# Network 1's last two blocks take seven block products for eight, and attention goes four heads by 512 tokens

## The chip, the cores and the metric

One core of a Trainium2 chip runs the whole program. The metric is the device time of one execution in microseconds (us); the median of three runs stands for a kernel. PE is TensorE, DVE VectorE, ACT ScalarE, POOL GpSimd, and SP the engine whose queue issues all transfers here.

## What is computed

```python
scores = scale * np.matmul(q_c, k_c.transpose(0, 1, 2, 4, 3))   # chunks of 64 tokens, 8 x 8 heads, head size 64
attn = softmax(scores)                                        # row maximum taken off, 1e-9 in the sum
x = np.matmul(attn, v_c)                                      # 4608 tokens x 512 after the transpose of heads
h = x @ w_in; r = np.maximum(h, 0.0); x = (r * r) @ w_out     # network 1, 512 -> 2048 -> 512
h = x @ w_in2                                                 # network 2, same sizes
g = (a0 + a1*h + a2*h**2 + a3*h**3) / (1 + |b0|*|h| + |b1|*h**2 + 1e-6)
out = g @ w_out2
```

## The kernel before

**Numbers and products.** All data is float32. Every operand of a large product is held as two parts, `hi` (rounded to fp32r) and `lo` (what is left), and `mm3` (L372 to L376) issues three matmuls of 128x512 for one product of parts: lo by hi, hi by lo, hi by hi. Making the two parts of a tensor costs a copy (`copy`, L198 on ACT, L200 elsewhere) and a subtraction (`split_lo`, L203).

**Steps.** The 4608 tokens are 9 blocks of 512 (`NBLK`), the 2048 columns of the middle are 16 tiles of 128 (`NF`). One step s is one block and one such tile. In the loop of network 1 a step is `mm_h` (four chunks of 128 of the 512 inputs by three matmuls, 12 in all, into a PSUM bank `h`), `act1` (relu and square on ACT, then `gh`, a copy, and `gl`, a subtraction, both on DVE as a rule), and two and a half steps later `mm_out1` (12 matmuls into the four banks `ACC`). The tile `r` between the square and the subtraction has one buffer, so that the next step's relu waits for this step's `gl`. There are two `h` banks. After 16 steps `evac1` copies the four banks out and `store1` writes them to DRAM.

**Attention** is laid between the steps in units of 256 tokens by 8 heads: transposes of q and k on DVE, 64 small matmuls for the scores (`mm_s`), the softmax on DVE and ACT, eight block transposes on DVE (`s_tr`), and 64 small matmuls for the result at the next unit (`mm_pv2`), whose output is split straight into the tile X of its block. Two units make a block, in the order of the blocks, one in about 8 steps.

**An order written by hand.** Each piece of work is put down by `at(t, fn, ...)` with a time t in steps (`MOVED` shifts some); `issue` sorts by t and each engine takes its own work in that order, so the order on an engine is fixed and a wait at its head holds all that is behind it. In the stretch from step 22 on, the weights of network 2 are split on POOL and stored (`w2_split`, `w2_sum`, `w2_sum_split`, `w2_store`), one pair of tiles in 12 steps.

**The held steps.** The products h of the last 20 steps of network 1 (`BACK`) are made ahead, two steps in the time of one, and their r kept in SBUF (`keep`); their `mm_out1` comes later.

**Pairs.** The first product of network 2 is taken for two blocks at a time. A unit of a pair covers two blocks by two tiles; the 512 inputs are cut in halves too, so it is a product of 2x2 blocks, made by seven block products (`mm_p`, 6 matmuls each) on sums of x and of w (`x2q`, `w2q` in DRAM) in place of eight. `UNIT_SEQ = "1o562o37o4o"` gives a unit's order on PE; each `o` is one outstanding `mm_out` of 12 matmuls. `q_fork` copies the bank of product 1 to a second bank, `q_s5` copies that of 5 to SBUF, `q_v` and `q_22` add (L926, L930). Four tiles come out of a unit and each goes through eleven operations (`tile_jobs`: abs, lin, id, q, wh, wa, ln, exp, wr, u, g). Blocks 0 to 7 of network 2 are four pairs; block 8 goes in the plain way at the end, then 20 outstanding `o`. In this part a planner (`plan`) sets the order: it gives each job a cost (`COST`), a due time and the jobs it needs, and takes the job with the earliest due time among those ready on an engine. The weights for each `o` lie in a ring of six pages, filled by `o_load` (L275) with both parts, after the `mm_out` six `o` earlier.

## Time and profile before

| | |
|---|---|
| runs | 1602.35 us median of 3 (1601.53 to 1603.12) |
| the profiled execution | 1602.25 us; its span 1600.4 us |
| PE busy | 1587.4 us of the span |
| DVE, ACT, POOL busy | 1075.1, 921.6, 772.7 us |
| granted clock of PE | full in all 40 slices of the span |

The span runs from the first to the last instruction. A matmul's recorded duration overlaps the next one's; how often one starts says more of the rate. A row of a group of instructions gives line, engine, operation, the tile written and those read, the count, the busy time, the mean of one, and the idle time of the engine ahead of it with what ended it.

### The profile page before, as it was taken

The numbers are of one execution on the slowest core, as the hardware profiler recorded it, in microseconds if no ns is written. First come the engines' busy times: TensorE is split into PE (matmuls) and PEld (weight loads), VectorE is DVE, ScalarE is ACT, GpSimd is POOL, SyncE is SP. The second block draws the span as 40 slices with busy tenths as digits, with TensorE's granted clock in tenths as the row PEclk, the third lists the DMA queues.
The fourth block names the chain that finished last, engine by engine and source line by source line (L and its number), as shares of the span: only waits on it lengthen the run. The fifth ranks groups of instructions, "written<-read, shape, count | busy, mean of one in ns | idle before, by whom it ended". The sixth has DMA issues, their size and how long they took to land.

```text
span 1600.4 us, 25717 instructions
## 1 busy us (share of the span) xinstructions
PE 1587.4 (99%) x9165; PEld 1313.8 (82%) x9165; DVE 1075.1 (67%) x1688; ACT 921.6 (58%) x1462; POOL 772.7 (48%) x737
## 2 busy tenths in 40 slices
PE   8999999999999999999999999999999999999998
PEld 7878888888888888888888888888888888888887
DVE  6886666765666666653067887787777777777640
ACT  5863343333333333334578887887888878777641
POOL 3640212123121312224368876877687856555554
PEclk9999999999999999999999999999999999999999
DMA  9854574354535445444988999989999996666544
GB/s 251 229 146 135 179 209 119 100 141 103 155 89 140 118 125 134 134 126 133 315 308 272 291 296 328 336 279 329 338 291 279 330 344 226 204 205 211 178 162 141
DMA packets 359567, 337.28 MB, mean 211 GB/s; under 512 B 195472, under 2 KB 269456, under 8 KB 358416
## 3 DMA queue, kind: packets, MB, share of 16 engines
q1 hardware_dynamic: 359440, 335.64, 67.9%
q8 instruction: 73, 1.20, 0.3%
q14 instruction: 54, 0.44, 0.1%
HBM read 253.76 MB, written 81.79 MB: 210 GB/s over the span
## 4 chain that ended last, share of the span: by engine, by line
PE 94%; DVE 3%; SPq 1%; ACT 1%; DMA 0%; issue 0%; POOL 0%; DVEq 0%; POOLq 0%; ACTq 0%
PE acc L374 16%; PE acc L376 16%; PE acc L375 16%; PE h L374 15%; PE h L376 15%; PE h L375 15%; PE h L592 1%; PE a L571 1%; DVE w L967 1%; SPq L662 1%; DVE spare L974 0%; DMA qn<-in_q_dram 0%; DVE w L954 0%; DVE w L950 0%; DVE h L971 0%
## 5 line engine op out<-in xcount | busy, mean ns | idle before, releaser
L374 PE MATMUL h<-x,w 128*128 128x512 f32 (+1 forms) x824 | 320.0, 388 | 0.6 <-ACT r L491 0.5
L375 PE MATMUL h<-x,w 128*128 128x512 f32 (+1 forms) x824 | 319.0, 387 | 0.3 <-DVE x L203 0.3
L376 PE MATMUL h<-x,w 128*128 128x512 f32 (+1 forms) x824 | 318.9, 387 | 0.0
L946 POOL TENSOR_TENSOR t<-t,r 128x512 f32<-128x512 f32 x144 | 188.3, 1308 | 135.1 <-ACT t L938 129.9
L374 PE MATMUL acc<-gh,w 128*128 128x512 f32 x576 | 226.2, 393 | 0.0
L376 PE MATMUL acc<-gh,w 128*128 128x512 f32 x576 | 224.3, 389 | 0.0
L375 PE MATMUL acc<-gl,w 128*128 128x512 f32 x576 | 224.2, 389 | 0.0
L374 PE MATMUL acc<-w,gl 128*128 128x512 f32 x575 | 223.7, 389 | 0.0
L375 PE MATMUL acc<-w,gh 128*128 128x512 f32 x575 | 223.7, 389 | 0.0
L376 PE MATMUL acc<-w,gh 128*128 128x512 f32 x575 | 223.7, 389 | 0.0
L203 POOL TENSOR_TENSOR gl<-spare,gh 128x512 fp32r<-128x512 f32 x146 | 191.3, 1316 | 54.3 <-ACT gh L198 48.2
L491 ACT ACTIVATE r<-h 128x512 f32<-128x512 f32 x124 | 73.8, 595 | 246.2 <-PE h L376 153.1
L200 POOL CAST st<-wc 128x512 fp32r<-128x512 f32 x32 | 21.2, 663 | 376.7 <-DVE wc L245 376.7
L374 PEld LDWEIGHTS h<-x,w 128*128 128x128 f32 x824 | 154.7, 188 | 32.7 <-ACT r L491 0.9
L375 PEld LDWEIGHTS h<-x,w 128*128 128x128 f32 x824 | 154.7, 188 | 31.9 <-DVE x L203 0.5
L376 PEld LDWEIGHTS h<-x,w 128*128 128x128 f32 x824 | 154.7, 188 | 31.6
L200 DVE CAST gh<-r 128x512 fp32r<-128x512 f32 x117 | 57.2, 489 | 149.8 <-ACT r L492 149.2
L950 DVE TENSOR_TENSOR w<-w,h 128x512 f32<-128x512 f32 x144 | 98.4, 683 | 67.1 <-ACT w L942 64.3
L374 PEld LDWEIGHTS acc<-gh,w 128*128 128x128 f32 x576 | 108.1, 188 | 23.3 <-POOL w L203 0.4
L376 PEld LDWEIGHTS acc<-gh,w 128*128 128x128 f32 x576 | 108.1, 188 | 22.7
L376 PEld LDWEIGHTS acc<-w,gh 128*128 128x128 f32 x575 | 107.9, 188 | 22.5
L374 PEld LDWEIGHTS acc<-w,gl 128*128 128x128 f32 x575 | 107.9, 188 | 22.4
(145 smaller groups left out, 3061.5 us busy)
## 6 DMA issues: line engine op xcount, KB each, us to landing
w<-w2o SPq DMA_DIRECT2D x144, 512.0 KB, 4.9
w<-w2q SPq DMA_DIRECT2D x256, 256.0 KB, 5.0
x2q<-xroom SPq DMA_DIRECT2D x24, 896.0 KB, 6.4
st<-in_moe_w_in_dram SPq DMA_DIRECT2D x32, 512.0 KB, 4.5
st<-in_moe_w_out_dram SPq DMA_DIRECT2D x32, 512.0 KB, 4.6
w2q<-st SPq DMA_DIRECT2D x32, 512.0 KB, 2.8
w<-x2q SPq DMA_DIRECT2D x30, 512.0 KB, 9.2
x<-x2q SPq DMA_DIRECT2D x26, 512.0 KB, 7.7
```

Source lines behind the costliest of these rows:

```text
L200: eng.tensor_copy(out=o, in_=x)
L203: eng.tensor_tensor(out=o, in0=x, in1=hi.bitcast(F32), op=ALU.subtract)
L374: nc.tensor.matmul(out=o, lhsT=al, rhs=bh, start=first and i == 0, stop=False, **kw)
L375: nc.tensor.matmul(out=o, lhsT=ah, rhs=bl, start=False, stop=False, **kw)
L376: nc.tensor.matmul(out=o, lhsT=ah, rhs=bh, start=False, stop=last and i == len(pairs) - 1, **kw)
L491: nc.scalar.activation(out=r, in_=ps, func=ACTF.Relu)
L571: nc.tensor.matmul(out=o[half(c), h, p], lhsT=q_[half(h), p, half(c)], rhs=k_[half(h), p, half(c)], start=True, stop=True)
L592: nc.tensor.matmul(out=o[c][half(h), i, p], lhsT=v_[half(c), 2 * p + h], rhs=a_[h][half(c), p] if t < 2 * TPB else a_[h][half(c), :, p], s ...
L662: nc.sync.dma_start(out=x[:, t], in_={"q": q, "k": k_in, "v": v}[nm][0, 4 * k:4 * k + 4, t0:t0 + 128, :].rearrange("h r d -> r h d"))
L946: nc.gpsimd.tensor_tensor(out=t, in0=t, in1=T["r", b, f], op=ALU.mult)
L950: nc.vector.tensor_tensor(out=w, in0=w, in1=T["H", b, f], op=ALU.mult)
L967: nc.vector.scalar_tensor_tensor(out=w, in0=w, scalar=co[:, 0:1], in1=T["r", b, f], op0=ALU.add, op1=ALU.mult)
```

## The change

Blocks 7 and 8 of network 1 (`NP1 = 1` pair) leave the loop of steps and become a fifth pair (`KP = 5`), the first of the planned part; their tiles get relu and square (`q_relu`, `q_sq`) instead of the eleven operations. The loop has 7 blocks, 112 steps (`NS1`), and its last 20 are the held ones. For this, network 1's first weights are needed as seven sums (`w1q`): POOL adds hi and lo together again, forms the sums and splits them, in eight portions. The input of the pair is needed unsplit in DRAM: `x1_raw` copies it out of the banks, `x1_store` writes it. The second weights of network 1 are kept as one sum (`w1r`) in place of two parts, so a ring page for a step below 144 is loaded at half the size and split again by `op_hi` (ACT) and `op_lo` (DVE). In the loop from step 30 the copy `gh` is on ACT, and the subtraction `gl` of odd steps on POOL, except where it is needed early. Attention units after the first become 512 tokens by 4 heads, 12 of them from step 29.55 to 92.55, with blocks 7 and 8 (units 28 to 34) ahead of some of the others. The last two portions of network 2's weights go into the planned part. The scratch tiles `e` share buffers with `q`, `ee` and others.

```diff
+NP1 = 1
+W2_EARLY = 6
+ATTN = [(29.55, 12), (34.55, 14), (40.55, 28), (45.55, 16), (50.55, 32), (56.55, 18), (61.55, 20), (66.55, 22), (72.55, 30),
+        (77.55, 34), (82.55, 24), (87.55, 26)]
+T_W1Q = [24 + 12 * i + x for i in range(4) for x in (4.1, 9.25)]
+T_W1R = [19.8, 21.0, 22.2, 76.1, 77.3, 78.5, 81.2, 84.0]
+GC_A = range(30, 92)
+GL_G = range(31, 92, 2)
...
+    NB1 = NBLK - 2 * NP1
+    NS1 = NB1 * NF
+    KP = NP1 + NBLK // 2
...
+    def w1q_sum(u):
+        raw = []
+        for i in range(2):
+            need("w", (0, 2 * u + i, 0), 4)
+            hi, lo = w_slot(2 * u + i, 0)
+            raw.append(tl("wc", [128, DM], I32, "wc").bitcast(F32))
+            nc.gpsimd.tensor_tensor(out=raw[i], in0=hi.bitcast(F32), in1=lo.bitcast(F32), op=ALU.add)
+        T["raw", u] = raw
...
+    def w1q_split(u, i):
+        if i:
+            st = T["sums1", u] = tl("attn", [128, DM, 2], I32, "ee")
+        x = s_view(T["sums1", u])
+        y = T.pop(("raw", u))[0].rearrange("p (k s j) -> p s k j", k=2, s=2) if i else x[:, 1].bitcast(F32)
+        copy(nc.gpsimd, x[:, 0], y)
+        split_lo(nc.gpsimd, x[:, 1], y, x[:, 0])
...
+        if NS1 - BACK + j < NS:
+            nc.sync.dma_start(out=o_page(j).bitcast(F32)[:, 1], in_=w1r[f // 2][:, f % 2])
+        else:
+            nc.sync.dma_start(out=o_page(j).bitcast(F32), in_=w2o[f // 2][:, f % 2])
+
+    def op_hi(j, eng):
+        stage("page_o", j, 0)
+        need("ring_o", j, 1)
+        copy(eng, o_page(j)[:, 0], o_page(j)[:, 1].bitcast(F32))
+
+    def op_lo(j, eng):
+        stage("page_o", j, 1)
+        o = o_page(j)
+        split_lo(eng, o[:, 1], o[:, 1].bitcast(F32), o[:, 0])
...
-        copy(on(f"gc{s}", "V"), g[0], r)
-        split_lo(on(f"gl{s}", "V"), g[1], r, g[0])
+        copy(on(f"gc{s}", "A" if s in GC_A else "V"), g[0], r)
+        split_lo(on(f"gl{s}", "G" if s in GL_G and s not in early else "V"), g[1], r, g[0])
...
+    def q_relu(b, f):
+        r = T["r", b, f] = keep("r", b * NF + f - NS1 + BACK)
+        nc.scalar.activation(out=r, in_=T.pop(("H", b, f)), func=ACTF.Relu)
+
+    def q_sq(b, f):
+        r = T.pop(("r", b, f))
+        nc.scalar.activation(out=r, in_=r, func=ACTF.Square)
...
-    for m in range(NBLK // 2):
+    for m in range(KP):
...
+        if b < NBLK:
+            e = job("A", COST["relu"], ready_, due - 20, q_relu, b, f)
+            made[b, f] = job("A", COST["sq"], [(e, 0)], due - 10, q_sq, b, f)
+            return [(e, E_LAT)]
...
+            page = [(made["ring", n], D_LAT)] if ("ring", n) in made else []
+            if N_PRE <= n and s < NS:
+                e = job("A", COST["hi"], page, due - 16, op_hi, n, nc.scalar)
+                page = [(job("V", COST["add"], [(e, E_LAT)], due - 8, op_lo, n, nc.vector), E_LAT)]
+            made[x] = job("PE", size["o"], deps + page, 0, mm_o, n)
```

**POOL in the loop of steps.** Before, the four sums of a portion of network 2's weights (L311) and the splits of the two sums, with nothing but weights around them (L200 is a copy, L203 a subtraction):

```order
L311 TENSOR_TENSOR st<-wc 128x256
L311 TENSOR_TENSOR st<-st,wc 128x256
L311 TENSOR_TENSOR st<-wc 128x256
L311 TENSOR_TENSOR st<-wc,st 128x256
L200 CAST st<-st 128x2x256
L203 TENSOR_TENSOR st<-st 128x2x256
L200 CAST st<-st 128x2x256
L203 TENSOR_TENSOR st<-st 128x2x256
```

The same place now (L386 the sums, L217 copies, L220 subtractions), with a step's `gl` inside and a portion of network 1's weights behind (L302 adds the parts, L312 forms the sums in the buffer `ee`):

```order
L386 TENSOR_TENSOR st<-wc 128x256
L386 TENSOR_TENSOR st<-st,wc 128x256
L386 TENSOR_TENSOR st<-wc 128x256
L386 TENSOR_TENSOR st<-wc,st 128x256
L217 CAST st<-st 128x2x256
L220 TENSOR_TENSOR st<-st 128x2x256
L220 TENSOR_TENSOR gl<-r,gh 128x512
L217 CAST st<-st 128x2x256
L220 TENSOR_TENSOR st<-st 128x2x256
L302 TENSOR_TENSOR wc<-w_12_88 128x512
L302 TENSOR_TENSOR wc<-w_13_89 128x512
L312 TENSOR_TENSOR ee<-wc 128x256
```

A step's `gl` now stands behind the weights' sums and their first split.

**ACT in network 1's pair.** Around the start of the pair's fifth unit (`h<-h` is `q_fork`, `s<-h` is `q_s5`, L1064 and L1068 are relu and square, `w_0<-w_0` and `w_4<-w_4` are `op_hi`, `gh<-spare` is the copy for an `o`):

```order
L1064 ACTIVATE spare_7057<-h 128x512
L1068 ACTIVATE spare_7057<-spare_7057 128x512
L215 ACTIVATE w_4_6874<-w_4_6874 128x512
L215 ACTIVATE gh<-spare_7133 128x512
L215 ACTIVATE w_0_7131<-w_0_7131 128x512
L215 ACTIVATE h<-h 128x512
L215 ACTIVATE w_0_7131<-w_0_7131 128x512
L215 ACTIVATE s_7910<-h 128x512
```

An `op_hi`, which waits for a page, now stands ahead of `q_fork`, and one ahead of `q_s5`.

**DVE in the first pair of network 2.** Before, around `q_v` and `q_22` of its third unit (L926, L930; the others are the tiles' operations):

```order
L974 SCALAR_TENSOR_TENSOR spare_8010<-h,w 128x512
L926 TENSOR_TENSOR h<-h,s_8747 128x512
L950 TENSOR_TENSOR w<-w,h 128x512
L954 SCALAR_TENSOR_TENSOR w<-w,co,h 128x512
L930 TENSOR_TENSOR h<-h,s_8747 128x512
L967 SCALAR_TENSOR_TENSOR w<-w,co,h 128x512
```

The same two sums in that pair's fourth unit now (L1056 and L1060; L220 is `op_lo`):

```order
L1112 SCALAR_TENSOR_TENSOR spare_6878<-h,w 128x512
L1056 TENSOR_TENSOR h<-h,s_9149 128x512
L220 TENSOR_TENSOR w_2_7153<-w_2_7153 128x512 x2
L220 TENSOR_TENSOR w_4_6874<-w_4_6874 128x512
L1088 TENSOR_TENSOR w<-w,h 128x512
L1060 TENSOR_TENSOR h<-h,s_9149 128x512
L1092 SCALAR_TENSOR_TENSOR w<-w,co,h 128x512
```

Three subtractions for pages stand between the two sums.

## Rows read from the trace of the kernel before

**Rows 1.** The page: busy time, share of the span and instructions of each engine.

```profile
PE 1587.4 (99%) x9165; PEld 1313.8 (82%) x9165; DVE 1075.1 (67%) x1688; ACT 921.6 (58%) x1462; POOL 772.7 (48%) x737
```

**Rows 2.** The page: the chain of work that ended last, share by engine.

```profile
PE 94%; DVE 3%; SPq 1%; ACT 1%; DMA 0%; issue 0%; POOL 0%; DVEq 0%; POOLq 0%; ACTq 0%
```

**Rows 3.** Busy time by stretch: start:end, length, engines, clock, DMA share, GB/s.

```profile
0.00:40.00 40.00, 33.53 (x448) 29.28 (x449) 27.69 (x46) 23.22 (x40) 15.02 (x19) 1.00 0.99 251
320.00:640.00 320.00, 320.00 (x2240) 265.08 (x2239) 210.58 (x374) 108.81 (x182) 74.95 (x77) 1.00 0.47 126
1520.00:1600.40 80.40, 76.27 (x340) 63.09 (x338) 19.81 (x30) 25.08 (x39) 40.39 (x38) 1.00 0.45 151
```

**Rows 4.** Who waited for whom, PE: us in total, times, longest.

```profile
PE h L374 <- DVE h L926: 1.0, 2, 0.8
PE h L374 <- ACT r L491: 0.5, 1, 0.5
```

**Rows 5.** Timeline of PE in the loop: start us, us, instruction.

```profile
332.18 0.39 PE L374 MATMUL h<-x,w 128*128 128x512 f32 x1
...
334.90 0.39 PE L374 MATMUL acc<-gh,w 128*128 128x512 f32 x1
...
337.71 1.16 PE L592 MATMUL h<-at,v 64*64 64x64 f32 x64
338.70 1.11 PE L571 MATMUL a<-k,q 64*64 64x64 f32 x64
339.74 0.50 PE L374 MATMUL acc<-gh,w 128*128 128x512 f32 x1
```

**Rows 6.** Groups of instructions by form, DVE and ACT, 320 to 640 us.

```profile
L203 DVE TENSOR_TENSOR gl<-r,gh 128x512 fp32r<-128x512 f32 x56 | 47.1, 841 | 1.9
L200 DVE CAST gh<-r 128x512 fp32r<-128x512 f32 x56 | 27.2, 485 | 71.0 <-ACT r L492 70.9
L245 DVE SCALAR_TENSOR_TENSOR wc<-wc,st 128x512 int32<-128x512 int32 x18 | 14.3, 795 | 1.1 <-ACT st L239 0.7 <-POOL st L203 0.2
L643 DVE TENSOR_TENSOR e<-e,z 128x512 f32<-128x512 f32 x14 | 12.9, 923 | 0.2
L491 ACT ACTIVATE r<-h 128x512 f32<-128x512 f32 x56 | 33.3, 595 | 124.5 <-PE h L376 73.2 <-DVE gl L203 42.1 <-issue 5.1
```

**Rows 7.** Timeline of POOL at one portion of network 2's weights.

```profile
392.82 0.84 POOL L311 TENSOR_TENSOR st<-wc 128x256 f32<-128x256 f32 x1 [11.05 <-DMA w2q<-st]
...
397.33 0.61 POOL L200 CAST st<-st 128x512 fp32r<-128x512 f32 x1
398.02 1.28 POOL L203 TENSOR_TENSOR st<-st 128x512 fp32r<-128x512 f32 x1
```

**Rows 8.** Timeline of PE just after it: the first matmul of a step's output.

```profile
404.69 0.39 PE L374 MATMUL acc<-gh,w 128*128 128x512 f32 x1
```

**Rows 9.** Busy time by stretch, first pair: one unit, four units, one unit.

```profile
797.00:817.40 20.40, 20.40 (x92) 16.89 (x91) 6.12 (x9) 12.22 (x20) 8.74 (x9) 1.00 0.95 368
817.40:899.00 81.60, 81.60 (x362) 67.57 (x361) 65.92 (x90) 66.79 (x103) 67.00 (x65) 1.00 0.86 271
919.40:939.80 20.40, 20.40 (x91) 16.89 (x91) 18.97 (x24) 15.71 (x25) 15.65 (x15) 1.00 0.91 287
```

**Rows 10.** Groups by form, DVE and ACT, 880 to 960 us.

```profile
L974 DVE SCALAR_TENSOR_TENSOR spare<-h,w 128x512 f32<-128x512 f32 x10 | 6.9, 692 | 0.3
L974 DVE SCALAR_TENSOR_TENSOR spare<-r,w 128x512 f32<-128x512 f32 x4 | 6.7, 1668 | 0.1
L971 DVE SCALAR_TENSOR_TENSOR r<-t,r 128x512 f32<-128x512 f32 x4 | 5.6, 1392 | 0.4
L198 ACT ACTIVATE gh<-spare 128x512 fp32r<-128x512 f32 x7 | 4.4, 625 | 0.0
```

**Rows 11.** The page loads (L275), 790 to 1300 us: issue to landing.

```profile
DMA to landing us min/median/max: 3.6/6.1/11.6
```

More of the change, by code (lines that the diff above doesn't have):

```diff
@@ new lines, in w1_store, with w1q_copy @@
+    def w1_store(i):
+        nc.sync.dma_start(out=w1r[i], in_=T.pop(("w1r", i)))
+    def w1q_copy(u):
+        for i in range(2):
+            need("w", (0, 2 * u + i, 0), 4)
+            for s in range(i == 0 or 2):
+                nc.sync.dma_start(
+                    out=wq[0][u][:, 2 * i + s].rearrange("p (t k j) -> p (t k) j", t=2, k=2),
+                    in_=W[0, 2 * u + i].bitcast(F32).rearrange("p t (k s j) -> p s (t k) j", k=2, s=2)[:, s])
+            stage("wq", (0, u, i), 0)
@@ L415, in w_out @@
         need("ring_o", j, 1)
+        if s < NS:
+            need("page_o", j, 2)
         stage("out_j", j, 0)
@@ L436, in mm_out2 @@
             for j in PARTS:
-                T["rest", j.start] = bank(role(NF // 2 * (NBLK // 2) - 1, "be"[j.start > 0]))
+                T["rest", j.start] = bank(role(NF // 2 * KP - 1, "be"[j.start > 0]))
                 mm3(T["rest", j.start][:, j], [(gi, [z[:, j] for z in w])], True, True)
@@ L482, in act1 @@
         ps = T.pop(("h", s))
-        r = r_p.tile([128, NB], F32, name="r", tag="r") if s < NS - BACK else keep("r", s - NS + BACK)
-        if s >= NS - BACK:
+        r = r_p.tile([128, NB], F32, name="r", tag="r") if s < NS1 - BACK else keep("r", s - NS1 + BACK)
+        if s >= NS1 - BACK:
             nc.scalar.activation(out=r, in_=ps, func=ACTF.Relu)
@@ L518, in load_tok, with load_v @@
         T[nm, t] = x
+    def load_v(t):
+        b, i = divmod(t, TPB)
+        h0 = 4 * (i // 2)
+        x = tl("attn", [128, 2, 4, D], F32, "v", f"v{t % 2}")
+        for c in range(2):
+            for off, n, bb, ss in runs(b * NB + 256 * (i % 2) + 128 * c, 128):
+                nc.sync.dma_start(out=x[off:off + n, c], in_=v[bb, h0:h0 + 4, ss:ss + n, :].rearrange("h p d -> p h d"))
+        T["v", t] = x.rearrange("p c h d -> p (c h) d")
     def load_qk(u, src, nm, hp):
@@ L614, in x2_lo, with x1_raw, x1_store @@
                     stage("x", t, i)
+    def x1_raw(c, *ts):
+        stage("xc", (ts[-1], c), 0)
+        if c == 0:
+            T["xraw"] = tl("attn", [128, 2, 512], F32, "xraw", "ee" if ts[0] == 34 else "vx")
+        x = T["xraw"].rearrange("d p (n c i) -> d c p n i", c=2, i=64)
+        copy((nc.scalar, nc.vector)[c], x[:, c], T["x2", ts[-1]][c])
+    def x1_store(*ts):
+        b, i = divmod(ts[0], TPB)
+        for c in range(2):
+            need("xc", (ts[-1], c), 1)
+        stage("x1", (b, i // 2), 0)
+        nc.sync.dma_start(out=x_rows(b)[:, i:i + 2], in_=T["xraw"])
     def s_max(t):
@@ L619, in s_max, with e_half @@
         nc.vector.tensor_reduce(out=m, in_=T["s", t], axis=AX.X, op=ALU.max)
+    def e_half(i):
+        if "ee" not in T:
+            T["ee"] = tl("attn", [128, 2, 512], F32, "ee")
+        return T["ee"][:, i]
     def s_sub(t):
@@ L1101, in attn_moe_moe_kernel @@
             break
+        before = t, t + 1
         at(t0, a_ps, t)
@@ L1130, in t_h @@
     def t_h(s):
-        return s if s < NS - BACK + 2 else NS - BACK + 2 + (s - NS + BACK - 2) * 0.5
-    for s in range(NS):
+        return s if s < NS1 - BACK + 2 else NS1 - BACK + 2 + (s - NS1 + BACK - 2) * 0.5
+    for s in range(NS1):
         if s < 2:
@@ L1146, in attn_moe_moe_kernel @@
     for i in range(NF // 2):
-        at(19.8 + 1.6 * i, w1_save, i)
+        at(T_W1R[i], w1_raw, i)
+        at(T_W1R[i] + 0.75, w1_store, i)
     for u in range(NF // 2):
+        at(20.4 + 1.6 * u, w1q_copy, u)
+        t = T_W1Q[u]
+        at(t, w1q_sum, u)
+        at(t + 0.6, w1q_sum2, u)
+        at(t + 1.2, w1q_split, u, 0)
+        at(t + 1.8, w1q_store, u, 0)
+        at(t + 2.4, w1q_split, u, 1)
+        at(t + 2.8, w1q_store, u, 1)
+    for u in range(W2_EARLY):
         t = 24.0 + 12.0 * u
@@ L1285, in x_jobs @@
+    if NP1:
+        for u in range(W2_EARLY, NF // 2):
+            w2_jobs(u, 340 * (u - W2_EARLY))
     def x_jobs(i, deps):
         m = i // 7
-        if m < NBLK // 2 and ("xq", 8 * m + 7) not in made:
+        if m < KP and ("xq", 8 * m + 7) not in made:
             later.setdefault(m, []).append((i, deps))
             return
-        deps = deps + ([(made["xq", 8 * m + 7], D_LAT)] if m < NBLK // 2 else [(made["st", NBLK - 1, k], D_LAT) for k in range(KC)])
-        due = nominal["p", m, 0, ORDER[i % 7]] if m < NBLK // 2 else nominal["s", 0]
+        deps = deps + ([(made["xq", 8 * m + 7], D_LAT)] if m < KP else [(made["st", NBLK - 1, k], D_LAT) for k in range(KC)])
+        due = nominal["p", m, 0, ORDER[i % 7]] if m < KP else nominal["s", 0]
@@ L1442, in attn_moe_moe_kernel @@
             issue(T_P2)
-        for nm, bufs in TB.items():
-            pool(ctx, "t" + nm, bufs)
         pool(ctx, "s5", 1)
@@ L1451, in attn_moe_moe_kernel @@
         T["more"] = tl("sx", [128, MORE, NB], F32, "more")
+        with ExitStack() as p2:
+            pool(p2, "w", 3)
+            pool(p2, "wc", 3)
+            issue(min(t for t, _, fn, _ in events if fn is q_abs))
+        for nm, bufs in TB.items():
+            pool(ctx, "t" + nm, bufs)
         issue(3 * NS)
```

271 lines of the change are left out of this document (180 added, 91 removed).

## The prediction

> **What bounds the kernel now.** I read the page first. PE is busy 1587.4 of 1600.4 us [rows 1], and the chain that ended last runs 94% on PE [rows 2], so the kernel is as long as PE's list of work plus its gaps. Where the 13.0 us of gaps lie is read from the busy time by stretch [rows 3]: 6.5 us in the first 40 and 4.1 in the last 80.4, none in the 320 us in the middle of network 1's loop. That leaves 2.4 us in between; the waits of PE name 1.0 of it as the sum `q_v` on DVE and 0.5 as a relu on ACT [rows 4]. So a matmul taken out of the middle is worth its full time, and any wait that is put there is paid in full. The price of a matmul is not its recorded 0.39 us: in the timeline [rows 5] twelve start between 332.18 and 334.90, 2.72 us, or 0.2267 each. The same rows give attention on PE: both products of a unit take 337.71 to 339.74, 2.03 us.
>
> The sum is made against the profiled execution, 1602.25 us, which is 0.10 below the median of the runs, 1602.35.
>
> **What goes away: 10.9 us.** Blocks 7 and 8 have 32 tiles of 12 matmuls, 384. As a pair they are 8 units of 7 products of 6, 336. The built order shows it: PE has 8015 instructions before and 7967 after, 48 fewer, and the small matmuls and transposes of attention are as many as before. 48 x 0.2267 = 10.9 us, all of it on the path, and no bank or page is added on PE's side. The attention units move earlier, and so do their 2.03 us, but they don't change.
>
> **What is added in the loop (steps 30 to 92): 0.8 us, bounds 0 to 8.** Twelve units now stand in 63 steps of 5.44 us (two times 2.72), with 24 us of attention about 367 us, where the old order gave a unit some 8 steps. DVE: of 210.6 us in 320 [rows 3] I take off the `gl`, `gh` and weight joins of rows 6 and divide by seven units: (210.6 - 47.1 - 27.2 - 14.3) / 7 = 17.4 us a unit. After: 12 x 17.4 = 209, 39 `gl` at 0.84 make 33, some 21 joins at 0.80 make 17; 259 of 367, 70% where 66% hid entirely. `gh` moves to ACT, 62 copies at 0.63 [rows 10], which brings ACT from 34% to under a half. POOL has the most to take: 23% of the time now [rows 3], which is 86 of 367 us; eight portions of `w1q` at 9.7 us (by the rows of POOL: two additions and two subtractions of 1.28, four half-size sums of 0.84, two copies of 0.61 [rows 7]), 23 `gl` at 1.28 and ten additions for `w1r` add 78, 29 and 13. That is 206, 56%. None is full; what matters is what a `gl` on POOL stands behind. At one portion of weights POOL waited 11.05 us for a store, and the first split ended at 399.3 [rows 7]. A `gl` of the third step of that portion, standing there as the order now has it, would end at 400.6, and PE took up that step's output at 404.69 [rows 8]: 4.1 us to spare. The single buffer `r` is held as long, and ACT already waited 42.1 us for it in 56 steps without PE noticing [rows 6]. On SP the loads of q and k fall from 640 to 448, and 40 transfers for `w1q` come in, 1451 instructions in all before and 1452 after; a unit's loads have about five steps, 27 us, instead of eight. I take 0.8 us, nearer to nothing, because the row has 4.1 us left; the upper bound is a POOL 5.5 us later than that at each of six portions, (5.5 - 4.1) x 6 = 8.4.
>
> **What is added in network 1's pair: 0.5 us, bounds 0 to 14.** ACT has a relu and a square where network 2 has five operations, so it has room, and DVE too. New is that `op_hi`, which waits for a page, stands in ACT's queue ahead of `q_fork`. Its load is issued after the `mm_out` six earlier, 24 matmuls or 5.4 us before product 1 ends; product 6, which needs the copy, comes 18 matmuls or 4.1 us after that. `op_hi` and `q_fork` take 0.6 us each, so PE idles only if a page lands later than 5.4 + 4.1 - 1.2 - 0.3 for the issue = 8.0 us after it is asked for. The median is 6.1, the longest 11.6 [rows 11]. Four units have this order: at worst 4 x 3.6 = 14 us. I take 0.5, as the median lies well inside.
>
> **What is added in the first pair of network 2: 1.7 us, bounds 0 to 26.** Here the last 20 outputs of network 1 meet the eleven operations on each tile, and each has an `op_hi` and an `op_lo` that the old kernel did not need. In the old first pair four units took 65.9 us of DVE and 66.8 of ACT in 81.6 [rows 9], 16.5 and 16.7 a unit of 20.4 us, and the unit before them 6.1 and 12.2. Four `op_hi` at 0.63 bring ACT to 19.2. `op_lo` subtracts two tiles of SBUF. Its nearest rows are DVE operations that read their main operands from SBUF or PSUM [rows 10]: 0.69 with one in PSUM, 1.39 and 1.67 with both in SBUF beside a busy POOL; a softmax multiplication with its main operands in SBUF took 0.92 in the loop [rows 6]. I take 1.0, so DVE needs 16.5 + 4.0 = 20.5 of 20.4: just full. A full unit was no stall at 18.97 of 20.4 [rows 9], the first of the five has 14 us free, and the pages at its start are split in the pair before. I take 1.7 us. The bounds: nothing, and five units at 18.97 + 4 x 1.67 - 20.4 = 5.25 us each, 26 us.
>
> The Trainium skill, "GPSIMD Engine Reference", section 8 (Key points), says that GpSimd shares its SBUF interfaces with VectorE and contends with DVE instructions that have two SBUF inputs. The 1.67 beside 0.69 in one stretch [rows 10] agrees with it. By that rule alone each `op_lo` costs the longer time, and the sum comes out at the first rival below.
>
> The rest is the same instructions in the same order on PE: the start, three later pairs, the last block and the end. 1602.25 - 10.9 + 0.8 + 0.5 + 1.7 = 1594.35 us, and 1594.4 for the median.
>
> **The rivals.** *DVE becomes the bound in network 2's first pair (slower).* If `op_lo` always costs 1.67, a unit needs 16.5 + 6.7 = 23.2, 2.8 over; five units lose 14 us: 1602.35 - 10.9 + 14 + 1.3 = 1606.8. It decides from 10.9 / 5 = 2.2 us a unit, an `op_lo` of 1.53 us. For it: both rows above 1.3, and the three `op_lo` between `q_v` and `q_22`, where the old PE waits already lay. Against: the unit of 18.97 contained these long operations and cost nothing, and the first unit is light.
>
> *POOL is late in the loop (no change).* With six portions each 1.4 us too late (8.4) and the other two terms (2.2), 1602.35 - 10.9 + 8.4 + 2.2 = 1602.1. For it: POOL more than doubles its work and a wait at its head holds `gl`. Against: the 4.1 us of the row, and that the steps ahead of a unit keep `gl` on DVE.
>
> *Pages land late (slower).* Four units at the longest landing: 1602.35 - 10.9 + 14 + 2.5 = 1608.0. It needs every one of them near the longest, so it is the least likely.
>
> *All of it is hidden.* No new wait, and the 0.5 us behind the relu goes because the step it hit is laid otherwise: 1602.35 - 10.9 - 0.5 = 1591.0. That is the low end of the forecast's own case, not a case of its own. That fewer matmuls are not issued is excluded by the order.
>
> **How the numbers follow.** A measurement of this kernel can tell 0.2%, 3.2 us, from no change; so faster is below 1599.1, slower above 1605.6. Forecast, new waits of up to 7 us: 0.72, all of it faster. DVE as the bound: 0.11, of which 0.03 faster, 0.02 within, 0.06 slower. POOL late: 0.11, of which 0.02 faster, 0.08 within, 0.01 slower. Pages late: 0.06, of which half within and half slower. That makes 0.77 faster, 0.13 within and 0.10 slower. The range goes from 1590.8, with every wait hidden, to 1601.5, which takes in the forecast's case and the milder part of the rivals; what is left above it is most of the 0.10 and about half of the 0.13.
>
> **What would show it.** Right: PE busy down by about 11 us in the page, the busy stretches of PE still full in the loop, PE's waits in the middle below 6 us in sum, and those there are behind DVE in network 2's first pair. Wrong in the loop: waits of PE for `gl` on POOL or for a relu on ACT behind it. Wrong in the pair of network 1: waits for `q_fork` with ACT waiting for a page. Wrong in the next pair: DVE over 95% busy in its first five units and PE waiting for `q_v` or `q_22`. If PE's busy time fell by much less than 10.9, the price of a matmul would be wrong.

## The result and the profile after

The changed kernel took 1611.9 us (median of four runs, 1609.0 to 1612.3), the kernel before 1601.95 on the same chip: ratio 1.0057, 95% interval 1.004 to 1.0075. It is slower by about 10 us, where 1594.4 was forecast and the range ended at 1601.5. The profiled execution of 1612.33 us has a span of 1610.6. In the rows, SPq stands for SP's queue of transfers, `ev`, `vx` and `xraw` for tiles that a copy out of PSUM fills.

The page of the changed kernel, busy time and the chain that ended last, which answer to [rows 1, 2]:

```profile
PE 1584.2 (98%) x9117; PEld 1305.9 (81%) x9117; DVE 1058.3 (66%) x1603; ACT 1009.0 (63%) x1612; POOL 998.8 (62%) x944
...
PE 75%; SPq 6%; POOL 5%; DMA 5%; DVE 4%; issue 3%; ACT 2%; POOLq 0%; DVEq 0%; ACTq 0%
```

The 48 matmuls are gone (9165 to 9117), but PE now idles 26.4 us instead of 13.0, and the chain leaves PE for a quarter of its length: for SP's queue, POOL, DMA and DVE. No engine but PE is over two thirds busy. So this is not a new bound, it is a set of waits. PE's busy time fell by 3.2 us only, not by 10.9; why is said with the reasons below.

Busy time by stretch after the change (columns as in [rows 3]):

```profile
160.00:320.00 160.00, 154.07 (x1137) 127.07 (x1136) 107.02 (x189) 60.88 (x103) 78.70 (x78) 0.98 0.68 184
320.00:640.00 320.00, 317.65 (x2401) 262.07 (x2400) 185.81 (x335) 156.03 (x256) 175.15 (x175) 1.00 0.69 197
830.00:920.00 90.00, 87.19 (x376) 69.46 (x375) 84.03 (x108) 75.38 (x120) 77.40 (x71) 1.00 0.79 246
```

and two of these stretches before it:

```profile
160.00:320.00 160.00, 159.50 (x1058) 131.76 (x1058) 106.92 (x197) 55.47 (x94) 34.47 (x36) 1.00 0.54 152
830.00:920.00 90.00, 89.93 (x397) 74.16 (x396) 70.82 (x98) 74.42 (x115) 78.14 (x75) 1.00 0.88 274
```

Two places lost: the loop from 160 us on, where PE's idle time from 160 to 320 us went from 0.5 to 5.9 us and the granted clock fell to 0.98 (and from 320 to 640 us, where it had none, to 2.35), and network 2's first pair, where DVE went from 70.8 to 84.0 of 90 us.

How much each lost is better read from marks than from idle time, since a matmul is recorded with 0.39 us where the next follows after 0.2267 [rows 5]: each gap looks up to 0.16 us shorter than it is. The marks are DVE's first sums (`q_v`) of network 2's first pair and of its second; PE has 48 matmuls fewer before the first, as it should, and as many behind it. Timeline of DVE, the kernel before, then the changed one:

```profile
806.92 0.70 DVE L926 TENSOR_TENSOR h<-h,s 128x512 f32<-128x512 f32 x1 [64.20 <-PE h L376]
...
971.46 0.69 DVE L926 TENSOR_TENSOR h<-h,s 128x512 f32<-128x512 f32 x1
```

```profile
810.62 0.70 DVE L1056 TENSOR_TENSOR h<-h,s 128x512 f32<-128x512 f32 x1 [12.97 <-PE h L451]
...
979.50 0.69 DVE L1056 TENSOR_TENSOR h<-h,s 128x512 f32<-128x512 f32 x1
```

With 10.9 us less of matmuls the first mark should stand at 796.0. It stands at 810.6: **14.6 us lost up to there** (start, loop and network 1's pair), where the forecast had 0.8 + 0.5. From the mark to the end it was 793.5 us and is 800.0: **6.5 us lost behind it**, where the forecast had 1.7; 4.3 of them lie between the two marks (164.5 to 168.9), the other 2.2 in what follows. 14.6 + 6.5 - 10.9 = 10.2, the difference of the spans.

What PE waits for after the change, 160 to 640 us, then 640 to 925 us (us in total, times, longest):

```profile
PE acc L450 <- DVE gl L220: 2.9, 1, 2.9
PE h L692 <- ACT r L570: 2.6, 1, 2.6
PE acc L449 <- DVE ev L217: 2.4, 3, 1.6
```

```profile
PE h L449 <- DVE h L1056: 1.8, 3, 0.7
PE h L449 <- DVE h L1060: 1.4, 2, 1.0
```

**The first gap.** The timeline of the changed kernel around it:

```profile
227.42 0.71 DVE L631 STREAM_TRANSPOSE k<-ks 128x512 f32<-128x512 f32 x1 [4.21 <-DMA ks<-in_k_dram]
...
228.64 0.67 DVE L631 STREAM_TRANSPOSE k<-ks 128x512 f32<-128x512 f32 x1
...
229.23 0.65 DVE L217 COPY ev<-acc 128x512 f32<-128x512 f32 x1
...
229.81 0.98 DVE L220 TENSOR_TENSOR gl<-r,gh 128x512 fp32r<-128x512 f32 x1
...
230.82 0.60 ACT L570 ACTIVATE r<-h 128x512 f32<-128x512 f32 x1 [4.80 <-DVE gl L220]
230.84 0.80 PE L450 MATMUL acc<-gl,w 128*128 128x512 f32 x1 [2.85 <-DVE gl L220]
...
231.87 0.63 PE L449 MATMUL acc<-gh,w 128*128 128x512 f32 x1
```

The page blames `gl` on DVE. But `gl` was only fifth in a row: DVE stood 4.21 us at a transpose whose k had not landed, and a transpose of q, one of k and an evacuation came ahead of `gl`. PE then pays twice: after the gap its matmuls are 0.43 us apart instead of 0.2267, until 233.9 (seven steps take 3.09 instead of 1.59), which is the lower of its clock's two levels, 1.2 GHz. The granted clock, the third number from the end, ahead of that spell and over it:

```profile
224.00:229.00 5.00, 3.50 (x15) 2.36 (x13) 1.58 (x3) 1.96 (x4) 4.84 (x6) 1.00 0.51 145
230.00:235.00 5.00, 4.16 (x15) 3.11 (x18) 2.08 (x3) 3.23 (x6) 2.55 (x3) 0.66 1.00 333
```

So a gap of 2.85 us cost 2.85 + 1.5. Why k was late, on SP's queue:

```profile
214.02 5.52 SPq L620 DMA_DIRECT2D ks<-in_k_dram  x8
219.58 1.61 SPq L291 DMA_DIRECT2D w1q<-w  x3
221.53 4.31 SPq L620 DMA_DIRECT2D ks<-in_k_dram  x8
```

The last k load was issued at 225.8, behind a portion of the new copies. The transfers themselves are hardly slower, though the DMA engines are busier: from 160 to 640 us a k load landed 2.4 us after its issue (median; 1.6 to 6.1), and 2.0 (1.6 to 6.0) before. It is the issue that comes late.

**The second gap**, 2.58 us at 302.2, hangs on a line that the diff does not touch. ACT's timeline in the changed kernel:

```profile
287.33 0.63 ACT L215 ACTIVATE gh<-r 128x512 fp32r<-128x512 f32 x1
296.78 0.20 ACT L1136 ACTIVATE co<-co 128x2 f32<-128x2 f32 x1 [8.82 <-DMA co<-in_moe_b_dram]
296.89 0.64 ACT L254 ACTIVATE wc<-st 128x512 f32<-128x512 f32 x1
...
297.98 0.58 ACT L570 ACTIVATE r<-h 128x512 f32<-128x512 f32 x1
```

The coefficients of network 2 are loaded and made positive at step 44 in both kernels. Before, the loads were issued at 268.0 and 268.5, and ACT read them at 279.7 without a wait:

```profile
268.53 0.43 SPq L997 DMA_DIRECT2D co<-in_moe_b_dram  x1
...
279.67 0.19 ACT L998 ACTIVATE co<-co 128x2 f32<-128x2 f32 x1
```

Now they are issued at 293.0, behind eight k loads, and ACT stands 8.82 us at an operation of 0.20 us that nobody needs for another 500 us, with a relu behind it.

### The profile page after: what moved, and what is told of

It reads as the page before. It is cut to its first block, busy times and chain, and to the rows that moved or that the text cites. A ratio compares the mean times of both kernels' runs of the same rounds, so it can differ in the third digit from the quotient of the medians.

```text
span 1610.6 us, 26091 instructions
## 1 busy us (share of the span) xinstructions
PE 1584.2 (98%) x9117; PEld 1305.9 (81%) x9117; DVE 1058.3 (66%) x1603; ACT 1009.0 (63%) x1612; POOL 998.8 (62%) x944
## 4 chain that ended last, share of the span: by engine, by line
PE 75%; SPq 6%; POOL 5%; DMA 5%; DVE 4%; issue 3%; ACT 2%; POOLq 0%; DVEq 0%; ACTq 0%
PE acc L449 13%; PE acc L450 13%; PE acc L451 13%; PE h L449 11%; PE h L450 11%; PE h L451 11%; SPq L620 3%; POOL t L1084 2%; POOL gl L220 1%; PE h L692 1%; POOL xroom L426 1%; SPq L792 1%; PE a L665 1%; DMA st<-in_moe_w_out_dram 1%; DMA w1q<-ee 1%
## 5 line engine op out<-in xcount | busy, mean ns | idle before, releaser
L449 PE MATMUL h<-x,w 128*128 128x512 f32 (+1 forms) x760 | 295.8, 389 | 3.0 <-DVE h L1056 1.8
L450 PE MATMUL h<-x,w 128*128 128x512 f32 (+1 forms) x760 | 294.1, 387 | 0.3 <-DVE x L220 0.3
L451 PE MATMUL h<-x,w 128*128 128x512 f32 (+1 forms) x760 | 294.1, 387 | 0.0
L220 POOL TENSOR_TENSOR gl<-spare,gh 128x512 fp32r<-128x512 f32 x174 | 232.1, 1339 | 79.4 <-ACT gh L215 75.3
L449 PEld LDWEIGHTS h<-x,w 128*128 128x128 f32 x760 | 142.7, 188 | 34.9 <-DVE h L1056 3.5
L450 PEld LDWEIGHTS h<-x,w 128*128 128x128 f32 x760 | 142.7, 188 | 29.2 <-DVE x L220 0.5
L451 PEld LDWEIGHTS h<-x,w 128*128 128x128 f32 x760 | 142.7, 188 | 29.2
L570 ACT ACTIVATE r<-h 128x512 f32<-128x512 f32 x92 | 54.7, 594 | 146.6 <-PE h L451 87.7
L220 DVE TENSOR_TENSOR w<-w 128x512 fp32r<-128x512 f32 x52 | 55.3, 1077 | 119.0 <-ACT w L215 118.9
L450 PEld LDWEIGHTS acc<-gl,w 128*128 128x128 f32 x576 | 108.5, 188 | 25.5 <-DVE gl L220 3.3
L449 PE MATMUL h<-w,w 128*128 128x512 f32 x320 | 125.3, 392 | 3.4 <-DVE h L1056 1.8
```

The lines of the kernel that those rows point to most:

```text
L220: eng.tensor_tensor(out=o, in0=x, in1=hi.bitcast(F32), op=ALU.subtract)
L449: nc.tensor.matmul(out=o, lhsT=al, rhs=bh, start=first and i == 0, stop=False, **kw)
L450: nc.tensor.matmul(out=o, lhsT=ah, rhs=bl, start=False, stop=False, **kw)
L451: nc.tensor.matmul(out=o, lhsT=ah, rhs=bh, start=False, stop=last and i == len(pairs) - 1, **kw)
L570: nc.scalar.activation(out=r, in_=ps, func=ACTF.Relu)
```

## The experiments

Three theories. **S**: transfers that SP issues late hold an engine that works in order, and PE pays the gap and a spell at half the clock. **P**: POOL, with the sums of `w1q` and half of the `gl`, is late. **F**: DVE and ACT are merely fuller. For network 2's pair, **V**: `op_lo` fills DVE. All ratios are to the kernel before, timed on the same chip.

**1. The coefficients' operation on ACT at step 70.**

```
     def init2():
         nc.sync.dma_start(out=co[:, 0:4], ...)
         nc.sync.dma_start(out=co[:, 4:6], ...)
+    def init3():
         nc.scalar.activation(out=co[:, 4:6], in_=co[:, 4:6], func=ACTF.Abs)
...
     at(44, init2)
+    at(70, init3)
```

> Only the absolute value of the coefficients on ACT is moved, from step 44 to step 70; the two transfers stay at step 44. Theory S (transfers that SP issues late hold an engine that works in order, and PE pays twice: the gap itself and then half the clock for a spell): the gap of 2.58 us at 302.2 and the slow spell behind it go, about 4.4 us: 1607.5 us, and the gaps near 231 and 333 stay. Theory P (POOL, with the sums of w1q and half of the gl, is late): ACT's wait for the coefficients had slack, no change, 1611.9. Theory F (DVE and ACT are simply fuller, so that any delay shows): the gap turns up elsewhere, 1610 to 1612.

1610.6 us (1606.9 to 1613.5), ratio 1.0043, interval 1.0026 to 1.006. Two settings of constants on DVE, 0.06 us each, move along with the operation. In the profile, which is the slowest of the four executions, the gap at 302 is gone, as S says; the one at 231 and those behind evacuations are there:

```profile
PE acc L449 <- DVE ev L217: 4.0, 2, 2.3
PE acc L450 <- DVE gl L220: 2.7, 1, 2.7
```

The median gained 1.3 us of the 4.4, within a spread of 6.6 us between runs: the gap is explained, the price is not settled here. In this execution the half-rate spell of the first gap is longer (a granted clock of 0.66 from 229 to 239 us), and another stands at 522.0 (0.83 from 516 to 526), where the changed kernel's profile has none.

**2. The copies into `w1q` behind the k loads.**

```
-        at(20.4 + 1.6 * u, w1q_copy, u)
+        at(ATTN[u + 1][0] - 0.85, w1q_copy, u)
```

> Only the copies of the weights into w1q (three transfers on SP for each of eight portions) are moved, from steps 20.4 + 1.6 u, between the loads of q and k, to 0.85 step before the second to ninth unit of the loop, behind those loads. Theory S: the k loads of the units at steps 34.55 to 40.55 are issued about 4 us earlier, the gap of 2.85 us at 230.8 and its slow spell go, about 4.5 us: 1607.4; the gap at 302 stays, that at 333 perhaps. Theory P: the sums of w1q are where they were, no change, 1611.9. Theory F: 1610 to 1612.

1613.2 us, ratio 1.0063 (1.0046 to 1.0079): no gain. PE's wait for `gl` on DVE near 231 is gone and only 0.29 us behind ACT is left there, so the copies did delay that k; but the waits behind evacuations rose from 2.4 to 4.7 us, the one behind the coefficients from 2.6 to 3.1, and PE waits for `gl` on POOL (1.5). What SP issues earlier for one is later for another.

**3. The loads of q and k closer together.**

```
-                    x = -0.5 + 0.1 * (t1 - t0) * j
+                    x = -0.5 + 0.06 * (t1 - t0) * j
```

> Only the loads of q and k in the loop are spread over 0.48 of the time between two units instead of 0.8, so that the last k load comes about 1.5 steps earlier in SP's order. Theory S: DVE's transposes of k no longer wait, the gaps at 230.8 (with its slow spell 4.5 us), 332.7 (1.55), 427 and 521 (0.8 together) go: about 1605; the gap at 302, behind the coefficients, stays, unless their transfers too come earlier (then about 1601). Theory P: no change, 1611.9. A danger for S: the earlier loads wait for DVE to free the tiles of the unit before, and SP holds what is behind them; then new gaps, up to 1616.

1630.7 us, ratio 1.0176 (1.0161 to 1.0191). Nothing but the order on SP was changed, and it cost 19 us: the danger named, in another form and worse than its 1616. DVE's wait for k did fall, from 28.6 to 14.0 us. But the stores of `w1q` now stand behind the loads, and POOL, which needs the buffer, waits for them: 54.2 us from 160 to 640 instead of 30.2. POOL, SP and ACT near 396 us:

```profile
390.84 7.64 SPq L324 DMA_DIRECT2D w1q<-ee  x2
...
396.18 0.61 POOL L217 CAST ee<-wc 128x512 fp32r<-128x512 f32 x1 [10.73 <-DMA w1q<-ee]
...
398.16 0.67 ACT L254 ACTIVATE wc<-st 128x512 f32<-128x512 f32 x1 [6.03 <-POOL ee L220]
```

and what PE waits for in that kernel:

```profile
PE h L692 <- ACT r L570: 10.7, 5, 3.9
PE acc L450 <- POOL gl L220: 7.3, 4, 2.8
```

**4. `gl` back on DVE.**

```
-GL_G = range(31, 92, 2)
+GL_G = ()
```

> Only the gl of every second step of the loop goes back from POOL to DVE. Theory P: POOL's lateness no longer reaches PE, and most of the 12 us lost in the loop come back: 1600 to 1604. Theory S: the gl at the gaps stood on DVE behind a transpose that waited for a k load; now every gl stands there, so no gain: 1611 to 1615. Theory F: DVE gets 23 more operations of about 0.84 us and the gaps grow: 1613 to 1620.

1614.4 us, ratio 1.0073 (1.0058 to 1.0089). A late `gl` on POOL, the way in which P was to reach PE, is out as the cause in the changed kernel: without a `gl` on POOL the gaps stand where they stood, at 232.8 (1.76), 303.2 (2.32), 333.8 (1.70). The time lies in the ranges of S and F both, so it does not tell these two apart.

**5. The pages of the old kernel**: both halves of network 1's second weights go to DRAM and come back, without `w1r` sums, `op_hi` and `op_lo`.

```
-    w1r = scratch("w1r", NF // 2, [128, 2, DM])
+    w1r = scratch("w1r", NF // 2, [128, 2, 2, DM])
...
-        nc.sync.dma_start(out=w1r[i], in_=T.pop(("w1r", i)))
+        nc.sync.dma_start(out=w1r[i], in_=WP[i].bitcast(F32))
...
-            nc.sync.dma_start(out=o_page(j).bitcast(F32)[:, 1], in_=w1r[f // 2][:, f % 2])
+            nc.sync.dma_start(out=o_page(j).bitcast(F32), in_=w1r[f // 2][:, f % 2])
...
-                e = job("A", COST["hi"], page, due - 16, op_hi, n, nc.scalar)
-                page = [(job("V", COST["add"], [(e, E_LAT)], due - 8, op_lo, n, nc.vector), E_LAT)]
```

> The second weights of network 1 are kept as in the old kernel: both halves of every page go to DRAM and come back, so the sums on POOL in the loop (16), and the 20 op_hi on ACT and 20 op_lo on DVE in the pairs, are gone; each page's transfer is twice as large. The loop's order is otherwise the same. Theory V (op_lo fills DVE in network 2's first pair, and op_hi and op_lo delay q_22 in network 1's pair): PE's gaps between 640 and 920 fall from 8.5 us to about 2, 6 to 7 us come back: about 1605.5. Rival D (the loads are the bound there: the DMA engines are busy 93% between 665 and 830, and ten of these pages more would be 2.5 MB more): PE waits for pages or products' tiles there, 1612 to 1620.

1605.0 us, ratio 1.0018 (1.0009 to 1.0028): 6.9 us better, the time that V gives. The edit also takes the 16 sums for `w1r` from POOL in the loop, so it is not V alone that it tests; nearer to V is the stretch between the two marks, 165.6 us instead of 168.9. (The change has 52 `op_hi` and 52 `op_lo`; the 20 in the expectation is a miscount.) The DMA share from 665 to 830 is 1.02 after 0.93, and PE waited there once, 0.33 us, for a tile of x: D does not decide. The loop is as bad as it was in this execution, with 4.7 us at the first gap.

**6. `op_lo` on POOL.**

```
-                page = [(job("V", COST["add"], [(e, E_LAT)], due - 8, op_lo, n, nc.vector), E_LAT)]
+                page = [(job("G", COST["lo"], [(e, E_LAT)], due - 8, op_lo, n, nc.gpsimd), E_LAT)]
```

> Only the engine of the op_lo planned in the pairs is changed, from DVE to POOL, at the planner's cost of a split on POOL. Theory V: DVE is free of them, the gaps behind q_22 in both pairs go, 5 to 6 us: about 1606.5, if POOL, 77.4 us busy in the 90 from 830, holds. Rival: POOL becomes what PE waits for there (12 more operations of about 1.3 us make 93 of 90), no gain or a loss: 1611 to 1618.

1624.7 us, ratio 1.0136 (1.0121 to 1.0151): the rival, and worse than its range. The busy time of a stretch, and PE's waits from 640 to 925 us:

```profile
830.00:920.00 90.00, 80.92 (x346) 65.01 (x345) 65.04 (x87) 73.74 (x115) 88.23 (x83) 0.98 0.75 233
```

```profile
PE acc L450 <- POOL gl L220: 9.5, 6, 3.4
```

DVE is down to 65.0 of 90, and POOL at 88.2 is the bound: `gl` comes late. So DVE was full because of `op_lo`, and POOL had no room either.

**7. The copies of `w1q` and the loads of v issued by ACT.**

```
-                nc.sync.dma_start(out=x[off:off + n, c], in_=v[bb, h0:h0 + 4, ...
+                nc.scalar.dma_start(out=x[off:off + n, c], in_=v[bb, h0:h0 + 4, ...
...
-                nc.sync.dma_start(out=wq[0][u][:, 2 * i + s]...
+                nc.scalar.dma_start(out=wq[0][u][:, 2 * i + s]...
```

> Only the queue of two kinds of transfers is changed: the copies of w1q and the loads of v in the loop are issued by ACT instead of SP. Theory S (SP, which in 160 to 640 issues for 351 us and waits in order for about 120 of 480, is the full resource of the loop): about 54 us of issue leave SP, the k loads come earlier without the loads being asked for earlier, and the gaps at 231 (4.5 with its slow spell), 333, 427 and 522 (2.4 together) go: about 1605; the gap behind the coefficients may go too (1601). Rival F (DVE, ACT and POOL are merely too full): ACT, 76 of 160 us busy, gets about 54 us more in 480 and the gaps behind its relu grow: 1612 to 1620.

1608.6 us, ratio 1.004 (1.0029 to 1.005): 3.3 us better than the change by the medians, though the two intervals overlap; the profile is the surer sign. DVE's wait for k fell from 28.6 us to 12.1, the first gap from 2.85 to 1.27, those at 427 and 522 went. The one behind the coefficients (2.11) and the one at 329 (1.36) stayed. F's harm on ACT did not come. But in network 1's pair PE now waits 2.16 us for `q_22` where it waited 0.96, with a granted clock of 0.93 from 640 to 665 us: part of what the loop gained is lost there in this execution.

**8. Edits 1, 6 and 7 together.**

> Three edits together: the absolute value of the coefficients on ACT at step 70; the copies of w1q and the loads of v on ACT's queue; op_lo of the pairs on POOL. If theories S and V hold and the terms add: 1611.9 - 4.4 - 7 - 5.5 = 1595, which would be faster than the kernel before by 0.4%. If one of them fails, about 1600; if ACT's queue does harm, above 1605.

1616.9 us, ratio 1.009 (1.0074 to 1.0105): edit 6 spoils it. Edits 1 and 7 take 7.8 us off edit 6 alone, about the sum of the 4.4 expected of edit 1 and the 3.3 measured for edit 7; the granted clock is 1.00 in all of the loop.

**9. The transposes of a unit's second tile 0.4 step later.**

```
-            t1 = t0 + (... else 0.8 * i - 1.7)
+            t1 = t0 + (... else 0.8 * i - 1.3)
```

On DVE this puts the evacuation and `gl` ahead of two transposes.

> Only DVE's transposes of q and k of the second tile of each unit move, by 0.4 step later; that puts them behind the evacuation of an accumulator and the gl that stand there at the end of a block. Theory S (what PE waits for stands behind transposes that wait for k): the three gaps behind evacuations (332.7, 427, 521: 2.4 us) go, and the one at 230.8 shrinks by the two transposes, 1.3 us, and with it perhaps its slow spell: 1607 to 1609. Against it: the tiles of q and k come free about 2 us later, SP's loads of the next unit wait at the head of its queue as in the run with the loads moved earlier, and other gaps grow: 1612 to 1620.

1614.2 us, ratio 1.0071 (1.0056 to 1.0087), in the range of the case against it. The gaps behind evacuations and the one behind `gl` on DVE are gone from PE's waits, as S says, but the time is no better: the wait behind the coefficients grew to 3.2 us and others came (0.7 and 0.3 for `gl` on POOL, 1.9 in network 1's pair, and there a clock of 0.93). DVE's wait for k is 31.3 us, not less.

**10 and 11. Edits 1, 5 and 7, and the same with edit 9.**

> Three edits: the absolute value of the coefficients on ACT at step 70, the copies of w1q and the loads of v on ACT's queue, and the second weights of network 1 as pages of both halves. If the terms add, 1605.0 - 4.4 - 3.3 = 1597.3, faster than the kernel before by 0.3%. Rival (the gaps of the loop replace each other, as in the run with the copies moved): 1601 to 1604, no change against before. A loss against before would need the DMA engines, which were over full share between 665 and 830 with these pages, to hold PE longer once it comes there earlier.

> The three edits of the run beside it and the transposes of the second tile 0.4 step later. If the terms add: 1597.3 less the gaps behind evacuations that are left, 2.2 us, is about 1595, faster than the kernel before by 0.45%; what would then be left of the change's 10.9 us is a loss of about 3.5 us. Rival: tiles free later, 1598 to 1604.

1597.2 us, ratio 0.9968 (0.9955 to 0.998), and **1595.8 us, ratio 0.9963 (0.995 to 0.9975)**: both beat both kernels, and both came out within 1 us of the sum of the terms. The second one's page, its marks, and what PE still waits for in the loop:

```profile
PE 1578.4 (99%) x9117; PEld 1303.7 (82%) x9117; DVE 1001.6 (63%) x1551; ACT 984.5 (62%) x1560; POOL 958.4 (60%) x928
```

```profile
799.91 0.70 DVE L1056 TENSOR_TENSOR h<-h,s 128x512 f32<-128x512 f32 x1 [12.97 <-PE h L451]
...
964.56 0.69 DVE L1056 TENSOR_TENSOR h<-h,s 128x512 f32<-128x512 f32 x1
```

```profile
PE acc L450 <- POOL gl L220: 0.7, 2, 0.4
...
PE acc L449 <- DVE ev L217: 0.5, 1, 0.5
```

Between the marks it is 164.65 us, as in the kernel before (164.54). The first mark is 3.9 us behind 796.0, and behind it 0.6 us are lost: of the 10.9 us, 6.4 are kept (1600.4 to 1594.0 in span). The clock is 1.00 in every stretch of the loop.

**12. Edits 1, 7 and 9 with the pages of the change.**

> The three edits of the loop alone (coefficients' absolute value on ACT at step 70, copies of w1q and loads of v on ACT's queue, transposes of the second tile 0.4 step later), with the pages of network 1 as the change has them. If loop and pages are separate losses that add, the best version so far (1595.8) plus the 6.9 us that the pages were worth alone: 1602.7, the kernel before within 0.2%. If the loop's edits only worked because POOL lost the 16 sums of those weights with the pages, the loop's gaps are back and it takes 1606 to 1611.

1605.1 us, ratio 1.0017 (1.0008 to 1.0026), 2.4 us above the sum and below the other case: 6.8 us better than the change, with the intervals apart. The profiled execution, the fastest of the eleven at 1601.6, has no gap above 0.33 us between 225 and 640, so the loop's gaps did not need the pages to go; the marks are 168.86 apart, as in the change. The other ten executions are up to 6.6 us longer; they have no profile, so whether gaps are left in them is not shown.

**13 to 15. Which edit of the loop carries it**, all with the pages of the old kernel (1605.0 alone): edit 1; edit 7; edits 1 and 9.

> Coefficients' absolute value at step 70, and the pages of the old kernel; SP's queue and the transposes as in the change. If the wait for the coefficients is worth its gap and slow spell: 1605.0 - 4.4 = 1600.6, with the gaps at 231 and 333 still there. If SP's queue alone carries the loss: about 1604.

> Copies of w1q and loads of v on ACT's queue, and the pages of the old kernel; the coefficients as in the change. If SP's queue is worth what it was alone: 1605.0 - 3.3 = 1601.7, with the gap of about 2.1 us near 300, behind the coefficients, still there. If it is worth the rest of the sum (7.8 - 4.4 = 3.4), the same.

> Coefficients and transposes moved, the pages of the old kernel; SP issues all transfers as in the change. If what counts is only what stands behind the transposes on DVE, SP need not be relieved: about 1596 to 1597, as the best version. If SP's queue is needed: the waits for k grow and gaps for gl on POOL or for relu on ACT take the place of those behind DVE, 1599 to 1603.

| with the pages of the old kernel | us | ratio, interval |
|---|---|---|
| nothing else | 1605.0 | 1.0018, 1.0009 to 1.0028 |
| 7 (ACT's queue) | 1603.8 | 1.0009, 1.0 to 1.0018 |
| 1 and 9 (coefficients, transposes) | 1601.4 | 0.9986, 0.9977 to 0.9995 |
| 1 (coefficients) | 1599.7 | 0.9987, 0.9978 to 0.9997 |
| 1 and 7 | 1597.2 | 0.9968, 0.9955 to 0.998 |
| 1, 7 and 9 | 1595.8 | 0.9963, 0.995 to 0.9975 |

The ratio is not that of the two medians (the fourth row shows it), so rows near each other are told apart by their intervals. Of the single edits here, only the misplaced wait for the coefficients stands clear of the noise: 5.2 us with SP's queue as in the change, which is its gap and slow spell and a little more, and 6.6 with the queue relieved. ACT's queue is worth 1.2 us without edit 1 and 2.5 with it by the medians, the same way as in edit 7, but each time the intervals overlap. For the transposes no gain is shown: 0.9986 beside 0.9987 without ACT's queue, 0.9963 beside 0.9968 with it. Without that queue DVE waits as long for k as with the old pages alone (35.3 and 35.6 us), and in 1 and 9 PE waits for `gl` on both engines:

```profile
PE acc L450 <- DVE gl L220: 2.0, 1, 2.0
PE acc L450 <- POOL gl L220: 1.9, 2, 1.5
```

In the best version DVE still waits 24.2 us for k in 8 times. What changed is that little of what PE needs stands behind it: PE's longest wait between 230 and 640 us is 0.5 us.

## Why the prediction failed, point by point

**What goes away, 10.9 us: right.** 48 matmuls fewer, and the best version's span is the old one less 10.9 plus 4.5 us, of which the marks put 3.9 ahead of network 2's first pair and 0.6 behind. By the prediction's own sign, a busy time of PE that falls by much less than 10.9 us, the price of a matmul would be wrong, and it fell by 3.2 (1587.4 to 1584.2). The price holds: in the best version, without slow spells in the loop, it fell by 9.0 (to 1578.4). In the changed kernel the two slow spells alone put back about 3.0 us of busy time, and the last matmul ahead of each gap is recorded with its whole 0.39; the rest is not traced.

**The loop, 0.8 us, bounds 0 to 8: this step failed.** Up to the first mark 14.6 us are gone, about 11 of them here: PE's idle time from 160 to 640 us grew by 7.8 us, and the two slow spells cost 3.0. The step looked at whether engines are full and at the 4.1 us that a `gl` on POOL had to spare. No engine became full, and edit 4 shows that a `gl` on POOL was not what held PE. The signs named for this step were waits of PE for `gl` on POOL or for a relu behind it; what came was a wait for `gl` on DVE behind a late k, and one for a relu on ACT behind the coefficients. The sentence that failed is the one on SP: that loads of q and k fall from 640 to 448, that 1451 instructions become 1452, and that a unit's loads have five steps instead of eight. It counted instructions and named no slack. The slack was in SP's own waits, 160 to 640 us, in the kernel before and in the changed one:

```profile
SPq L528 <- DVE q L538: 65.5, 8, 18.0
SPq L321 <- POOL st L203: 44.4, 10, 7.5
```

```profile
SPq L418 <- DMA x1q<-room: 26.2, 6, 8.0
SPq L324 <- POOL ee L220: 25.5, 8, 5.9
SPq L620 <- DVE q L631: 21.7, 7, 7.6
```

Issuing took about 350 us of these 480 in both (an estimate, the sum of the rows of SP's timeline). The first of the later rows, 26.2 us, lies wholly behind 540 us, where no gap is; what counts is the stretch ahead. From 160 to 540 us SP waited 118.6 us in all before and 89.9 now, and from 160 to 300, the stretch with the late k at 227 and the late coefficients, 45.7 before and 21.3 now. Before, SP's largest wait was for a tile of q to come free: it stood ready up to 18 us before that. Now that wait is a third as long (from 160 to 300 us 6.4 instead of 26.8), and SP waits for sums and splits on POOL with loads behind. The order of instructions was known beforehand and the old waits stood in the trace: that the loads might reach their readers late could have been asked of this row, and no price was put on it.

**What was not in the sum at all:** the coefficients at step 44. Their lines do not change, so no price was asked for, and they cost 5.2 us (edit 13) because the queue in front of them did change. Nor was the clock: the gaps of 2.58 and 2.85 us cost 1.5 more each in slower matmuls.

**Network 1's pair, 0.5 us, bounds 0 to 14: about 1 us, inside.** The cause is the one that was named, a page that lands late: this one was asked for at 644.18 and landed 9.1 us later, where the prediction allowed 8.0. It reached PE another way, not through `q_fork` but through `q_22`. ACT stands at `op_hi` for its page, DVE at `op_lo` for ACT, and `q_22` (L1060) behind both, with a join of network 2's weights between, which the change put into this part and which waits for ACT too:

```profile
653.35 0.63 ACT L215 ACTIVATE w<-w 128x512 fp32r<-128x512 f32 x1 [4.67 <-DMA w<-w1r]
...
654.02 0.69 DVE L220 TENSOR_TENSOR w<-w 128x512 fp32r<-128x512 f32 x1 [5.42 <-ACT w L215]
...
655.75 0.69 DVE L1060 TENSOR_TENSOR h<-h,s 128x512 f32<-128x512 f32 x1
```

It showed as 0.96 us of idle, once.

**Network 2's first pair, 1.7 us, bounds 0 to 26: right mechanism, wrong size, 4.3 us between the marks and up to 2.2 behind them.** PE waited for `q_v` and `q_22`, as named, with DVE 93% busy from 830 to 920 us. The term that was mis-sized is `op_lo`, taken at 1.0 us. Groups of DVE, 830 to 920 us, by form:

```profile
L220 DVE TENSOR_TENSOR w<-w 128x512 fp32r<-128x512 f32 x14 | 17.9, 1312 | 0.0
...
L1112 DVE SCALAR_TENSOR_TENSOR spare<-h,w 128x512 f32<-128x512 f32 x11 | 7.6, 692 | 0.4
```

1.31 us each, between the 1.0 taken and the 1.67 of the rival, and DVE was never idle ahead of them. Five units at 16.5 + 4 x 1.31 = 21.7 us, 1.3 over the 20.4, would be 6.7; the first unit with room takes one away, 5.4. The best version, without `op_lo` in this pair, has 5.9 of the 6.5 us back. What sets the size can be read off the changed kernel's `op_lo` one by one: the 8 with no work on POOL beside them took 0.69 us each, the one at 654.02 above among them, and the 34 with POOL at work for over 90% of their time 0.68 to 1.78, 1.22 on average. The rule of the Trainium skill ("GPSIMD Engine Reference", section 8, Key points), by which GpSimd contends with DVE instructions of two SBUF inputs, fits this row: 1.31 beside 0.69 with one input in PSUM, POOL 77.4 of 90 us busy.

**The rivals.** *DVE as the bound* named this loss, at 14 us instead of 4.3: it had every `op_lo` at 1.67. *POOL late* was not it (edit 4), but edit 3 shows it a transfer away. *Pages late* happened once. That the time came out slower, as two of the rivals had it, is no merit of theirs: together they account for about 5 of the 21 us lost. The chance of 0.10 for slower was built on these prices only. None of the rivals was a late load in the loop, though that was the place with the most new transfers.

Left open: why edit 1 gave 5.2 us with the old pages and 1.3 with the new ones, where runs spread over 6 us; what is left in single executions of edit 12; where all of the 3.9 us ahead of the first mark lie that the best version still loses (PE's idle time up to there is 2.0 us longer than before); and where behind the second mark the last 2.2 us of the change lie, of which 1.7 go with the pages (631.1 us from there to the end, 629.4 in the best version, 628.9 before). The best version without the edit of the transposes is not told apart from it by their intervals.
